# A reworked opening for a windowed-attention and feed-forward kernel: masks, row sums, key placement and loads of the first chunks

## The chip, the cores and the metric

The kernel runs on one NeuronCore of a Trainium2 chip. The core has engines that run side by side, each with its own queue of instructions taken in order: TensorE (PE, matrix products, with weight loads shown apart as PEld), VectorE (DVE), ScalarE (ACT), GpSimd (POOL) and SyncE (SP), which here only issues data transfers (DMA). SBUF is the working memory of 128 partitions; PSUM is the small memory into which TensorE writes.

The metric is device time in microseconds (us) of one execution. Times of instructions come from a profile of one execution; L275 is line 275 of the kernel's file.

## What is computed

```python
# attention: q, k, v are (8, 8, 576, 64) float32
scores = (1.0 / np.sqrt(64)) * np.matmul(q, k.transpose(0, 1, 3, 2))
mask = np.abs(pos[:, None] - pos[None, :]) <= 32
scores = np.where(mask, scores, -1000000000.0)
attn = np.exp(scores - np.max(scores, axis=-1, keepdims=True))
attn = attn / (np.sum(attn, axis=-1, keepdims=True) + 1e-09)
attn_out = np.matmul(attn, v)
# feed-forward on the 4608 tokens, heads side by side: x is (4608, 512)
h = x @ w_in            # (512, 2048)
g = np.maximum(0.01 * h, h)
out = g @ w_out         # (2048, 512)
```

Each token attends to the 65 tokens at most 32 positions away.

## The kernel before, in words

**Tiling.** Two heads form a pair (4 pairs per batch) and fill the 128 partitions together, 64 each. A batch of 576 tokens is cut into two halves of 288; a *chunk* i is one half of one pair, so there are 8 chunks per batch (0 to 3 the first half of pairs 0 to 3, 4 to 7 the second half) and 64 in all. Keys and values stand in block-diagonal buffers `kbd` and `vbd` (two of each, one per batch parity): per pair 9 blocks of 64 tokens, each 128 x 128 with one head in the upper left and the other in the lower right; the rest must be zero.

**One chunk.** `score(i)` multiplies key blocks with transposed queries into the PSUM tile `ps` (five matmuls, L275), ACT takes the exponential into `e` (L280), GpSimd multiplies with a mask of ones and zeros into `prob` (L282). `sums(i)` multiplies with a block-diagonal of ones, which gives the row sums already spread over the 64 partitions of a head (two matmuls, L304), and DVE takes the reciprocal of the 128 x 288 result (L309). `product(i)` multiplies with the value blocks into `x` (L320), and `scaled(i)` multiplies `x` with the reciprocals into `xT` (DVE, L334). `ps`, `s` and `x` have one PSUM buffer each, so the next chunk waits for the reader of the last.

**Feed-forward.** A *group* g is 288 tokens, 16 in all. `h_tile(g, f)` makes one 128-wide tile of h by four matmuls (L348), one for each pair's 128 columns of x, and ACT applies the leaky rectifier into `gT` (L355). `h_first` makes the first four tiles of a group with the pairs outermost, so that it can start before all pairs' `xT` are there. `o_tile(j)` makes 128 rows of the output by 16 matmuls (L390), evicted by ACT (L395) and stored through SP.

**Order of the work.** The order is written out by hand: every engine runs its instructions in the order of the program text, waiting on semaphores. For batches 0 and 1, q and k are cast to bf16 (`cast_qk`, L197), transposed on TensorE (`transposes`, L225) and evicted by ACT (L233 for q, L239 for k); `place_keys` then copies the keys into their blocks with DVE (L258). From batch 2 on, transposes are DMAs. Batch 0's q, k and v are all issued on SP (L79, L91), in the order q0 k0 q1 k1 v0 q2 k2 q3 k3 v1 v2 v3; after eight outstanding DMAs the next one waits for the first to land. The weights come in four chunks each through GpSimd's queue (L448, L452), cast to bf16 on the way. `keep_busy` (L402) issues matmuls whose result nobody reads.

The opening mixes casts, transposes, scores, sums and products of chunks 0 to 3 with the first feed-forward tiles. Batch 1's loads are released by a one-element memset on GpSimd (L75, `behind`), because SP would otherwise issue them early. `second_half` runs chunks 4 to 7 between the tiles of group 0. `second_pair(p)` transposes pair p of batch 1 between tiles of group 1 and, by `turn` (a counter of slots of four output matmuls), between the first output matmuls; from there a list of due times, `due`, decides in which slot the next chunk's `step` is placed.

Of the kernel before, what the change touches and what calls it, by code (L numbers as in the profile page):

```python
# [9 lines left out]
FP32 = mybir.dt.float32  # L10
# [6 lines left out]
def kernel(  # L17
# [50 lines left out]
    def load_qk(b, p, behind=None):  # L68
# [3 lines left out]
        for into, src, name in ((qf, q, "qf"), (kf, k, "kf")):  # L72
# [5 lines left out]
            if b < BY_DMA:  # L78
                nc.sync.dma_start(out=t, in_=heads.rearrange("a (p c) d -> p a (c d)", c=RUN))  # L79
            else:  # L80
                nc.sync.dma_start(
                    out=t.rearrange("p a (g e) -> p a g e", g=3),
                    in_=heads.rearrange("a (g p c) d -> p a g (c d)", g=3, c=2),
                )
            into[b, p] = t

    def load_v(b, p):

        t = fload.tile([128, NB, D], FP32, name=f"vf{p}")
        for a in range(2):  # L90
            nc.sync.dma_start(  # L91
                out=t[64 * a:64 * a + 64],
                in_=v[b, 2 * p + a].rearrange("(c p) d -> p c d", p=64),
            )
        vf[b, p] = t

    load_qk(0, 0)
    load_qk(0, 1)
    load_v(0, 0)
    load_qk(0, 2)  # L100
    load_qk(0, 3)
    for p in range(1, NPAIR):
        load_v(0, p)
# [33 lines left out]
    clear(vbd[0], 2)  # L137
# [20 lines left out]
    nc.gpsimd.memset(vbd[0][:, 3], 0.0)  # L158
    win_f = win.rearrange("p c m i -> p c (m i)")

    def make_mask(hf):
# [4 lines left out]

    NPROB = 6
# [5 lines left out]
    nc.scalar.activation(  # L173
        out=ps[:, 512:512 + HALF], in_=zero.to_broadcast([128, HALF]), func=AF.Copy,
    )
# [23 lines left out]
    def cast_v(b, p, on_act=False):  # L199
        for a in range(2):  # L200
            r = slice(64 * a, 64 * a + 64)
            if on_act:
                nc.scalar.activation(out=vbd[b % 2][r, p, :, r], in_=vf[b, p][r], func=AF.Copy)  # L203
            else:
                nc.gpsimd.tensor_copy(out=vbd[b % 2][r, p, :, r], in_=vf[b, p][r])  # L205
# [12 lines left out]
    def transposes(b):  # L218

        qT[b] = attn.tile([128, NPAIR, S], BF16, name="qT")  # L220
        for p in range(NPAIR):
            for which, src in (("q", qb), ("k", kb)):
# [14 lines left out]
                else:  # L237
                    kT = kt.tile([128, S], BF16, name="kT")
                    nc.scalar.activation(  # L239
                        out=kT.rearrange("p (i c) -> p i c", c=RUN),  # L240
                        in_=tp.rearrange("p c i -> p i c"), func=AF.Copy,
                    )
                    unplaced.append((b, p, kT))
                yield

    unplaced, landing = [], []

    def place_keys():

        while landing and landing[0][0] <= state["done"]:  # L250
            unplaced.append(landing.pop(0)[1:])
        while unplaced:
            b, p, kT = unplaced.pop(0)
            for a in range(2):
                r = slice(64 * a, 64 * a + 64)
                to = kbd[b % 2][r, p, :, r]
                if b < BY_DMA:
                    nc.vector.tensor_copy(out=to, in_=kT[r].rearrange("p (n j) -> p n j", j=64))  # L258
                else:
                    nc.vector.tensor_copy(  # L260
                        out=to.rearrange("p n (m c) -> p n c m", c=2),
                        in_=kT[r].rearrange("p (c n m) -> p n c m", c=2, n=NB),
                    )
# [6 lines left out]
    def score(i):  # L270
        b, hf, p = where(i)
        by_c = qT[b][:, p].rearrange("p (c i) -> p c i", c=2)
        for n_, blocks in enumerate(WIN[hf]):
            for blk, i0, n in blocks:
                nc.tensor.matmul(  # L275
                    ps_v[:, n_, :, i0:i0 + n], kbd[b % 2][:, p, blk],
                    by_c[:, :, hf * EVEN + i0:hf * EVEN + i0 + n], start=True, stop=True,
                )
        e = attn.tile([128, 2 * HALF], BF16, name="e")
# [15 lines left out]
    def sums(i):  # L295
# [14 lines left out]
        probs[i][2] = r  # L310

# [57 lines left out]
    def h_first(g):  # L369

        hs = [mmps.tile([128, 512], FP32, name="mm", tag="mm") for _ in range(4)]
        yield hs[0]
        for c in range(DMC):
            for f in range(4):
                h_mms(g, f, hs[f], (c,))
            if c == DMC - 1:
                for f in range(4):
# [19 lines left out]

    def keep_busy(t, lo, n):


        for _ in range(n):
            nc.tensor.matmul(  # L402
                t[:, lo:lo + 224], ones_bd, mask[0].rearrange("p n c i -> p (n c i)")[:, 0:224], start=False, stop=False,
                skip_group_check=True,
            )
# [14 lines left out]
    def step():  # L420
# [7 lines left out]
        weighted(i)  # L428
# [218 lines left out]
```

## Time and profile before

| | us |
|---|---|
| runs (three) | 318.51, 319.07, 320.56; median 319.07 |
| profiled execution, whole | 320.23 |
| its span, first to last instruction | 318.5 |
| PE busy | 303.2 (95%) |
| DVE busy | 218.2 (69%) |
| POOL busy | 191.6 (60%) |
| ACT busy | 182.6 (57%) |
| reciprocals L309 | 125.2, 64 of 1956 ns |
| mask multiplies L282 | 81.5, 64 of 1274 ns |
| SP and DMA: q or k load of 288 KB, issue to landing (median) | 4.5 and 5.0 |

The profile's page cuts the span into 40 slices and gives each engine's busy share in tenths, lists the chain of work that ended last, groups instructions by line with mean duration and the idle time ahead of them, and lists DMA issues. The timeline gives instructions in order of time: start, duration, engine, line, what is written from what. In the chain, "issue" is time in which an engine waited for nothing that the profile shows, SPq is SP's queue, and "DMA kf" is time until a transfer of keys landed.

### The profile page before, as it was taken

The page shows a single profiled execution, that of the slowest core. Times are in us where ns is not written, and L with a number is a line of the kernel's source. Part 1 is how long each engine was busy: PE and PEld are TensorE (multiplying, and loading weights), DVE is VectorE, ACT ScalarE, POOL GpSimd, SP SyncE. Part 2 cuts the span into 40 slices and gives each one's busy share as a digit, 9 for nine tenths or more (in the row PEclk, how much of TensorE's full clock was granted, in tenths as well). Part 3 has the DMA queues.
Part 4 walks back from the last instruction along what each step waited for, and adds up shares of the span by engine and source line. Part 5 has one row for each costly group of instructions (what it writes and reads, how often), then busy time and mean ns, then how long its engine had stood idle before and what let it go on. Part 6 is the DMA issues. An engine that isn't in the chain of part 4 may idle for free.

```text
span 318.5 us, 6474 instructions
## 1 busy us (share of the span) xinstructions
PE 303.2 (95%) x2449; PEld 204.3 (64%) x2449; DVE 218.2 (69%) x259; ACT 182.6 (57%) x393; POOL 191.6 (60%) x251
## 2 busy tenths in 40 slices
PE   2679998999999999999999999999999999999996
PEld 1467774585765858576765858576665858576653
DVE  5678955869655997688755997688745988565100
ACT  7577698474652828374652828375552837464531
POOL 7798963974546866686546866586637866330000
PEclk9999999999999999999999999999999999999999
DMA  8999999997999995399735995399733430000101
GB/s 179 211 186 218 267 250 203 250 206 181 216 242 196 231 206 150 82 251 203 155 76 127 238 227 136 75 223 232 162 76 104 109 70 33 35 35 2 66 31 71
DMA packets 108400, 49.46 MB, mean 155 GB/s; under 512 B 68816, under 2 KB 103888, under 8 KB 108368
## 3 DMA queue, kind: packets, MB, share of 16 engines
q1 hardware_dynamic: 104144, 44.84, 66.8%
q0 software_dynamic: 4224, 4.19, 8.0%
q8 instruction: 19, 0.31, 0.4%
q14 instruction: 13, 0.11, 0.1%
HBM read 36.70 MB, written 9.44 MB: 145 GB/s over the span
## 4 chain that ended last, share of the span: by engine, by line
PE 89%; DMA 3%; DVE 2%; SPq 1%; POOL 1%; ACT 1%; issue 1%; DVEq 0%; ACTq 0%
PE mm L348 39%; PE mm L390 38%; PE x L320 5%; PE ps L275 4%; DMA kf<-in_k_dram 3%; PE s L301 2%; DVE r L309 2%; SPq L79 1%; POOL w_in_bf L448 1%; DVE xT L334 1%; PE tp L225 1%; PE s L304 1%; ACT vbd L203 0%; SPq L91 0%; POOL prob L282 0%
## 5 line engine op out<-in xcount | busy, mean ns | idle before, releaser
L309 DVE RECIPROCAL r<-s 128x288 f32<-128x288 f32 x64 | 125.2, 1956 | 56.5 <-PE s L301 53.3
L282 POOL TENSOR_TENSOR prob<-e,mask 128x576 bf16<-128x576 bf16 x64 | 81.5, 1274 | 87.8 <-ACT e L280 41.1
L348 PE MATMUL mm<-xT,w_in_bf 128*128 128x288 bf16 x1024 | 134.0, 286 | 0.3
L390 PE MATMUL mm<-w_out_bf,gT 128*128 128x512 bf16 (+2 forms) x592 | 130.4, 373 | 0.2 <-DMA w_out_bf<-in_moe_w_out_dram 0.2
L355 ACT ACTIVATE gT<-mm 128x288 bf16<-128x288 f32 x256 | 101.4, 412 | 24.8 <-PE mm L348 8.5
L348 PEld LDWEIGHTS <-w_in_bf 128*128 128x128 bf16 x1024 | 98.4, 98 | 24.8 <-issue 0.6
L390 PEld LDWEIGHTS <-gT 128*128 128x128 bf16 x592 | 56.3, 98 | 59.6 <-issue 0.3
L395 ACT ACTIVATE o_sb<-mm 128x512 f32<-128x512 f32 (+2 forms) x37 | 21.7, 586 | 92.0 <-PE mm L390 92.0
L280 ACT ACTIVATE e<-ps 128x576 bf16<-128x576 f32 x64 | 41.4, 648 | 9.4 <-PE ps L275 9.2
L197 POOL CAST kb<-kf 96x384 bf16<-96x384 f32 (+1 forms) x56 | 35.5, 656 | 4.6 <-DMA kf<-in_k_dram 4.6
L205 POOL CAST vbd<-vf 64x576 bf16<-64x576 f32 x50 | 34.5, 689 | 1.8 <-DMA vf<-in_v_dram 0.4
L334 DVE TENSOR_TENSOR xT<-x,r 128x288 bf16<-128x288 f32 x64 | 29.3, 458 | 8.2 <-PE x L320 1.2
L260 DVE COPY kbd<-kT 64x576 bf16<-64x576 bf16 x48 | 32.3, 672 | 0.3
L275 PE MATMUL ps<-qT,kbd 128*128 128x128 bf16 (+2 forms) x320 | 26.5, 215 | 1.8 <-DVE kbd L258 1.2
L275 PEld LDWEIGHTS <-kbd 128*128 128x128 bf16 x320 | 21.0, 100 | 10.6 <-DVE kbd L258 1.5
L320 PE MATMUL x<-prob,vbd 128*128 128x128 bf16 (+2 forms) x320 | 26.0, 213 | 1.3 <-ACT vbd L203 0.7
L197 POOL CAST qb<-qf 96x384 bf16<-96x384 f32 x48 | 24.5, 538 | 0.0
L320 PEld LDWEIGHTS <-vbd 128*128 128x128 bf16 x320 | 20.6, 99 | 3.9 <-ACT vbd L203 1.8
L292 DVE TENSOR_TENSOR both<-prob 128x288 bf16<-128x288 bf16 x52 | 19.7, 380 | 0.9
L301 PE MATMUL s<-both,ones_bd 128*128 128x288 bf16 x52 | 14.9, 286 | 0.0
L258 DVE COPY kbd<-kT 64x576 bf16<-64x576 bf16 x16 | 7.1, 444 | 8.7 <-ACT kT L239 8.6
L225 PE MATMUL tp<-ident,qb 96*128 96x96 bf16 x48 | 4.4, 243 | 6.2 <-DVE qb L197 6.2
(43 smaller groups left out, 86.6 us busy)
## 6 DMA issues: line engine op xcount, KB each, us to landing
qf<-in_q_dram SPq DMA_DIRECT2D x32, 288.0 KB, 4.5
kf<-in_k_dram SPq DMA_DIRECT2D x32, 288.0 KB, 5.0
vf<-in_v_dram SPq DMA_DIRECT2D x64, 144.0 KB, 4.2
out_dram<-o_sb SPq DMA_DIRECT2D x35, 256.0 KB, 3.6
w_in_bf<-in_moe_w_in_dram POOLq DMA_DIRECT2D x4, 512.0 KB, 8.6
w_out_bf<-in_moe_w_out_dram POOLq DMA_DIRECT2D x4, 512.0 KB, 16.8
qT<-qb SPq DMA_TRANSPOSE x24, 4.1
kT<-kb SPq DMA_TRANSPOSE x24, 3.2
```

Source lines behind the costliest of these rows:

```text
L197: eng.tensor_copy(out=to, in_=tok)
L205: nc.gpsimd.tensor_copy(out=vbd[b % 2][r, p, :, r], in_=vf[b, p][r])
L260: nc.vector.tensor_copy(out=to.rearrange("p n (m c) -> p n c m", c=2), in_=kT[r].rearrange("p (c n m) -> p n c m", c=2, n=NB),)
L275: nc.tensor.matmul(ps_v[:, n_, :, i0:i0 + n], kbd[b % 2][:, p, blk], by_c[:, :, hf * EVEN + i0:hf * EVEN + i0 + n], start=True, stop=True,)
L280: nc.scalar.activation(out=e, in_=ps[:, P0:P0 + 2 * HALF], func=AF.Exp, scale=scale)
L282: nc.gpsimd.tensor_mul(pr.rearrange("p n c i -> p (n c i)"), e, mask[hf].rearrange("p n c i -> p (n c i)"),)
L309: nc.vector.reciprocal(r, s)
L320: nc.tensor.matmul(x_v[:, :, i0:i0 + n], vbd[b % 2][:, p, blk, :], pr[:, n_, :, i0:i0 + n], start=(blk == parts[0][1]), stop=(blk == parts ...
L334: nc.vector.tensor_mul(place(i), x, r)
L348: nc.tensor.matmul(h[:, 0:HALF], w_in_bf[:, c, ts(f, 128)], xT[:, c, ds(g * HALF % RING, HALF)], start=(c == 0), stop=(c == DMC - 1),)
L355: nc.scalar.activation(out=gT[:, f, ds(g * HALF % RING, HALF)].rearrange("p (i c) -> p i c", c=2), in_=h[:, 0:HALF].rearrange("p (c i) -> ...
L390: nc.tensor.matmul(o[:, lo:hi], gT[:, f, ds(128 * j % RING, 128)], w_out_bf[:, f, lo:hi], start=(f == 0), stop=(f == FFC - 1),)
```

## The change

All of it concerns the first two batches.

- **Loads.** Batch 0's queries go on SP, its keys on ACT's queue; its values follow, first blocks 0 to 4 of all pairs, then blocks 5 to 8. Batch 1's sixteen loads move in the text from the middle of the opening to after group 0.
- **Masks.** For chunks 0 to 3 TensorE first writes a tile `outside` (0 inside the window, -1e9 outside) into `ps` through an identity matrix, then adds the scores to it; the exponential goes straight into `prob`. From chunk 4 on GpSimd multiplies as before.
- **Row sums.** For chunks 0 to 3 `prob` is the stationary operand and two columns of ones move, so that sums come out by token row (96 rows, 6 columns); DVE takes the reciprocal of 96 x 6, copies it out 64-fold in fp32 (`wide`), and three fp32 matmuls with an identity turn it back into 128 x 288, which ACT copies to SBUF.
- **Keys.** For batches 0 and 1 the transposed keys are evicted from PSUM into their blocks directly, one head by ACT, the other by DVE.
- **Order.** The opening is rewritten, `keep_busy` is gone, the first `h_first` makes three tiles, value casts of batch 0 are all on GpSimd in two parts, two of the clears of `vbd` move to DVE. Batch 1's transposes and the first due times move to later slots, and chunks 9 to 11 have their sums made a step earlier.

```diff
-    load_qk(0, 0)
-    load_qk(0, 1)
-    load_v(0, 0)
-    load_qk(0, 2)
-    load_qk(0, 3)
-    for p in range(1, NPAIR):
-        load_v(0, p)
+    for p in range(NPAIR):
+        load_qk(0, p, k_eng=nc.scalar)
+    NB1 = NB // 2 + 1
+    for p in range(NPAIR):
+        load_v(0, p, 0, NB1)
+    for p in range(NPAIR):
+        load_v(0, p, NB1, NB)
...
+    make_mask(0)
+    outside = const.tile([128, 2, HALF], BF16)
+    nc.vector.tensor_scalar(
+        out=outside.rearrange("p n t -> p (n t)"),
+        in0=mask[0].rearrange("p n c i -> p (n c i)"),
+        scalar1=1e9, scalar2=-1e9, op0=ALU.mult, op1=ALU.add,
+    )
...
-                    kT = kt.tile([128, S], BF16, name="kT")
+                    nat = tp.rearrange("p c i -> p i c")
                     nc.scalar.activation(
-                        out=kT.rearrange("p (i c) -> p i c", c=RUN),
-                        in_=tp.rearrange("p c i -> p i c"), func=AF.Copy,
+                        out=kbd[b % 2][0:64, p, :, 0:64], in_=nat[0:64], func=AF.Copy,
                     )
-                    unplaced.append((b, p, kT))
+                    nc.vector.tensor_copy(out=kbd[b % 2][64:128, p, :, 64:128], in_=nat[64:128])
...
+        if i < NPAIR:
+            for n_ in range(2):
+                nc.tensor.matmul(
+                    ps[:, ds(P0 + n_ * HALF, HALF)], ident, outside[:, n_], start=True, stop=False,
+                    skip_group_check=True,
+                )
...
+        if i < NPAIR:
+            pr = prob[:, i % NPROB]
+            nc.scalar.activation(
+                out=pr.rearrange("p n c i -> p (n c i)"), in_=ps[:, P0:P0 + 2 * HALF],
+                func=AF.Exp, scale=scale,
+            )
+            probs[i] = [pr, None, None]
+            return
...
+    def sums_flat(i):
+        pr = probs[i][0].rearrange("p n c i -> p n (c i)")
+        sT = mmps.tile([128, 512], FP32, name="mm", tag="mm")
+        for c in range(3):
+            for n in range(2):
+                nc.tensor.matmul(
+                    sT[0:96, ds(2 * c, 2)], pr[:, n, ds(96 * c, 96)], ones_bd[:, 0:128:64],
+                    start=(c == 0 and n == 0), stop=True, skip_group_check=True,
+                )
+        rT = recip.tile([96, 3, 2], FP32, name="rT")
+        nc.vector.reciprocal(rT.rearrange("p c a -> p (c a)"), sT[0:96, 0:6])
+        wide = recip.tile([96, 3, 2, 64], FP32, name="wide")
+        nc.vector.tensor_copy(out=wide, in_=rT.unsqueeze(3).to_broadcast([96, 3, 2, 64]))
+        probs[i][1] = wide
+    def sums_spread(i):
+        wide = probs[i][1]
+        r = xps.tile([128, HALF], FP32, name="s")
+        for c in range(3):
+            nc.tensor.matmul(
+                r[:, ds(96 * c, 96)], wide[:, c].rearrange("p a d -> p (a d)"),
+                ident_f[0:96, 0:96], start=True, stop=True,
+            )
+        probs[i][2] = recip.tile([128, HALF], FP32, name="r")
+        nc.scalar.activation(out=probs[i][2], in_=r, func=AF.Copy)
...
     cast_qk(0, 0, nc.vector)
-    make_mask(0)
+    first_pair()
+    nc.vector.memset(vbd[0][:, 2], 0.0)
     cast_qk(0, 1, nc.vector)
     first_pair()
+    load_w_in(0, 512)
+    score(0)
+    nc.vector.memset(vbd[0][:, 3], 0.0)
+    cast_qk(0, 2, nc.vector)
     first_pair()
...
+    sums_flat(0)
+    cast_qk(0, 3, nc.vector)
+    load_w_in(512, 1024)
+    make_mask(1)
+    sums_spread(0)
+    sums_flat(1)
+    score(2)
+    first_pair()
+    sums_spread(1)
+    cast_v(0, 0, n1=NB1)
+    sums_flat(2)
+    product(0)
+    scaled(0)
     score(3)
+    sums_spread(2)
+    cast_v(0, 1, n1=NB1)
     product(1)
     scaled(1)
+    h0 = h_first(0, 3)
+    next(h0)
+    next(h0)
+    sums_flat(3)
+    load_w_in(1024, 1536)
+    cast_v(0, 2, n1=NB1)
     product(2)
     scaled(2)
+    next(h0)
+    sums_spread(3)
+    cast_v(0, 3, n1=NB1)
+    score(4)
+    product(3)
+    scaled(3)
+    load_w_in(1536, 2048)
+    next(h0)
+    load_w_out(0)
+    next(h0)
+    cast_v(0, 0, n0=NB1)
+    score(5)
     load_w_out(1)
     load_w_out(2)
+    cast_v(0, 1, n0=NB1)
+    load_w_out(3)
     score(6)
+    cast_v(0, 2, n0=NB1)
+    cast_v(0, 3, n0=NB1)
...
     second_half()
+    for p in range(NPAIR):
+        load_qk(1, p, nc.gpsimd if p == 0 else None)
+    for p in range(NPAIR):
+        load_v(1, p)
...
-        if f in (7, 11):
-            second_pair((f - 7) // 4)
+        if f == 14:
+            second_pair(0)
...
-    due = [O_US * n for n in (4, 7, 10, 12)]
+    due = [O_US * n for n in (10, 12, 14, 15)]
...
-        if turn == 1:
-            second_pair(2)
-        if turn == 2:
-            score(9)
-        if turn == 4:
-            second_pair(3)
+        if turn in (2, 6, 9):
+            second_pair({2: 1, 6: 2, 9: 3}[turn])
+        if turn in (3, 5):
+            score(8 + turn // 4)
+        if turn == 9:
+            sums(8)
+        if turn == 10:
             cast_v(1, 0, on_act=True)
```

## The prediction

> **What bounds the kernel now.** I read the page first, then the chain of waits in order of time, then the timeline of the first 65 us. From the page:
>
> ```profile
> PE   2679998999999999999999999999999999999996
> DMA  8999999997999995399735995399733430000101
> PE 89%; DMA 3%; DVE 2%; SPq 1%; POOL 1%; ACT 1%; issue 1%; DVEq 0%; ACTq 0%
> ```
>
> TensorE is full in every slice but the first four (8 us each) and the last. 89% of the chain is TensorE, so behind the opening a microsecond is worth one only where TensorE is made to wait. The chain through the opening:
>
> ```profile
> 5.83 9.66 DMA kf<-in_k_dram
> ...
> 15.54 0.82 POOL kb L197
> 16.36 2.35 POOL w_in_bf L448 x3
> ...
> 20.52 1.97 DVE r L309
> ...
> 23.91 1.88 DVE r L309
> ...
> 26.39 0.65 PE mm L348 x4
> ```
>
> The last keys land at 15.5; then GpSimd casts, issues three weight loads and masks; then VectorE's reciprocals follow each other until the fourth chunk of the first group can be multiplied at 26.39. These are what the change attacks. The timeline gives the durations I use (start, length, engine, line):
>
> ```profile
> 6.94 0.56 DVE L197 CAST qb<-qf 96x768 bf16<-96x768 f32 x1 [1.27 <-DMA qf<-in_q_dram]
> 7.78 0.91 DVE L258 COPY kbd<-kT 64x576 bf16<-64x576 bf16 x2 [0.28 <-ACT kT L239]
> 16.97 0.65 PE L275 MATMUL ps<-qT,kbd 128*128 128x96 bf16 x5
> 20.32 0.40 PE L275 MATMUL ps<-qT,kbd 128*128 128x96 bf16 x5
> 25.72 0.09 POOL L75 MEMSET qf<- 1x1 f32 x1
> 31.93 4.06 POOL L540 MEMSET kbd<- 128x1152 bf16 x4
> 64.16 1.63 PE L348 MATMUL mm<-xT,w_in_bf 128*128 128x288 bf16 x12
> ```
>
> To be seen: the second pair's query cast (6.94) runs before the first pair's keys are placed (7.78); the same five matmuls take 0.65 before about 19 us and 0.40 after; the memset that lets batch 1's loads go (25.72) stands six microseconds ahead of the long memsets of the other block buffers (31.93); from 64 us on (third group) the chain is TensorE without a gap.
>
> **What the Trainium skill says.** *TensorE: Matmul & The Clock Gate*, Part 1: the array runs at half clock until one window of about 3.4 us was busy. The trace agrees (0.65 against 0.40), though the clock row shows full speed. *DMA: Bandwidth & Descriptors*, Issuing engines are not separate DMA queues: a second issuing engine saves issue time only. The trace has 0.40 to 0.45 per q or k issue and shows no second ring. *FP8 and Floating Point Precision*, TensorE Precision Notes: true fp32 takes 4 passes; no fp32 matmul is in this trace. As prices: a VectorE read from PSUM is (120 + elements)/0.96 ns (*VectorE: DVE Perf Modes*, The TRN2 errata), 0.43 for the 288-element multiply that the trace shows at 0.46; a weight load is columns/1.2 ns (clock-gate page, LDWEIGHTS), 107 for 128 columns against 98 in the trace.
>
> **Method.** I walk the queues: each engine takes its instructions in program order, each starts 0.05 after the last thing it needs (cast ends 5.67, transposes start 5.72). Six transposes, or five score or value matmuls, take 0.48 of the array at half clock and 0.66 to their end (0.25 and 0.41 at full). Others, from the timeline: ACT eviction or exp 0.65, 0.43 for a gT; full reciprocal 1.96; multiply 0.46; mask multiply on GpSimd 1.27. Done for the kernel before with its own landing times, the walk puts the first group's fourth chunk at 26.5 (trace 26.39) and the third group at 64.7 (63.95).
>
> **The change part by part.**
>
> *Loads.* Keys go on ACT's queue, values after all of q and k. In the trace the first six microseconds of q and k move at 250 to 275 GB/s, later ones nearer 220: about 1.1 per 288 KB, plus some 1.7 to the signal. From 2.1, pair p is in at 2.1 + 2.2(p+1) + 1.7: 6.0, 8.2, 10.4, 12.6. Pair 0 comes later than before (queries 4.65), since two rings share the same engines; pair 3 three microseconds earlier. ACT's four issues push its table load and two clears to 6.1, which still precedes its first eviction.
>
> *Keys straight into blocks.* ACT's full eviction (0.65) plus two VectorE copies (0.91) become an ACT half (576 elements, 0.65) and a VectorE half from PSUM: (120 + 576)/0.96 = 0.72, an estimate from the page's price; 0.45 is its floor (one copy of today), 0.9 its top. But VectorE's half waits for ACT's half, and behind it in VectorE's queue stand a memset (0.5, a quarter of the 1.98 for 2304 elements) and the *next* pair's query cast, which before stood ahead. So each pair costs a whole round: cast 0.67, transposes 1.19 to their end, ACT 0.7, VectorE 0.77, memset 0.52, gaps 0.1: 3.95. Transposes start at 6.7, 10.6, 14.6 instead of 5.73, 7.55, 13.21. Landings no longer matter after pair 0.
>
> *Masks on TensorE.* Two 288-column matmuls per chunk (0.48 cold) ahead of the scores; GpSimd's 1.27 and its queueing go. Exp 0 ends at 13.4, against a masked result at 12.73 before.
>
> *Sums by token row.* Six small matmuls (weight load of 96 columns, 0.08 each: 0.5), reciprocal of 6 and broadcast copy of 384 (0.5 together, scaled from the 0.56 cast), three fp32 matmuls, ACT copy 0.4 replace two matmuls and the 1.96 reciprocal. The fp32 part: from below 0.3 (as bf16), from above 12 passes of 107 + 80 = 2.2; I take 1.1 (96 columns x 12 / 1.2 GHz, plus some loads). In sum a latency of 2.5 to 3, no shorter than 2.6 before; VectorE is freed of 1.5 each.
>
> *The fourth pair.* Its transposes stand on TensorE behind chunk 0's spread, which needs its broadcast (17.8), behind chunk 1's sums and chunk 2's scores: 20.4. Then ACT 22.4, VectorE 23.2, masks and scores 23.9, exp 24.6, sums 26.2, broadcast 26.8, spread 28.1, copy 28.6, multiply 29.1: fourth chunk at 29.2, 2.8 later than 26.39. The dummy matmuls are gone, but the array is dense from 18.7, so I take full clock from 22 (16 gives -0.5, 28 gives +1.6).
>
> *The order behind it.* Score 6 stands right behind score 5 and ahead of tile 3, and waits for an exp that ACT runs after three gT: tile 3 starts at 31.5. Before reached the same place at 27.17 with 0.73 more done (tile 3 and one sum): 5.1 behind. Then chunk 5's sums wait 1.0 for chunk 4's reciprocal, chunk 6's wait 1.5 for GpSimd, whose queue now has w_out issues (0.80 each) and second-half value casts between the masks: the second group starts at 42.8 instead of 35.2, 7.6 behind.
>
> *Batch 1's loads.* The memset that frees SP for them now comes after GpSimd's last mask (41.3) and six memsets (6.1): 47.5 instead of 25.8. All sixteen loads of q, k and v move past the weights on SP. First queries land 4.2 later; their cast ends at 52.4, and TensorE, ready at 50.5, waits 2; the keys cost 1.2 more, the next pair 0.6, and the four attention steps, squeezed between the last 24 output matmuls (24 x 0.216 = 5.2) though each needs 2.4 of VectorE, 2 to 3. Third group at 76.7 against 64.7 in the same walk: **12.0 later**. Nothing in the gap-free part after it gives this back, and it has the same work.
>
> The sum against the profiled execution: span 318.5 + 12.0, with 1.7 around it (320.23), is 332.2; that execution lies 1.2 above the median, so 319.07 + 12.0 = **331.1**.
>
> **Rivals.** Within 1% (3.2 us) cannot be told from no change.
>
> 1. *Same mechanism, cheap new operations*: fp32 at 0.3 per spread, VectorE half at 0.45, sums at 0.3, clock full from 16. Third group at 71.1, +6.4: 325.5. For it: no row excludes any of the five. Against: five favourable values at once.
> 2. *Dear new operations*: 2.2 per spread, 0.9 half, sums 0.8, cast 0.9, full clock only at 28: third group at 84.7, +20: 339. For it: weight loads of fp32 may not overlap, and the dummies were there to warm the array.
> 3. *Faster, through the loads*: today's chain has 9.66 on the last keys. Were the landings what holds the pairs, pair 3 at 12.6 instead of 15.5, less the reciprocals' 4 x 1.5 on VectorE and with no mask hop, would bring chunk four some 3.5 forward: 315.6. It decides if the round per pair falls below the 2.2 between landings; the queues give 3.95, so this needs VectorE's half not to wait for ACT and its cast to run ahead, which the program order excludes.
> 4. *No effect*: the opening loses what later slack returns. The trace has only about 1.5 of waiting between 27 and 64 us, so there is no such slack: 319.
>
> **Chances.** Forecast 0.62, cheap 0.17, dear 0.13, loads 0.05, no effect 0.03. Faster 0.05, within 1% 0.03, slower 0.92. The range runs from the cheap case's edge, 325, to 338, just short of the dear bound.
>
> **What would show it.** Transposes of pairs 1 and 2 near 10.6 and 14.6, led by VectorE; pair 3's after 19; fourth chunk of the first group at 27 to 31; a TensorE gap before score 6; batch 1's first q load issued after 45; third group at 71 to 82. I am wrong if VectorE's casts run ahead of ACT's evictions, if pairs follow the landings, or if batch 1's loads are out before 40.

## The result, and the profile after

Over four runs each the changed kernel takes 337.56 us (median) and the kernel before 319.35: 1.057 times as long, with a 95% interval of 1.050 to 1.064. The forecast was 331.1 with a range to 338.0, so the median lies 0.4 inside the range's end, and two of its four runs (338.47, 339.44) lie outside. The profiled execution of the changed kernel took 338.47 and has a span of 336.8.

The page of the changed kernel, TensorE's and the transfers' busy tenths and the share of the chain of waits by engine:

```profile
PE   1598797978999999899999999999999999999995
DMA  8990989999999999929993499559952521010101
PE 77%; POOL 6%; DVE 4%; DMA 4%; issue 4%; ACT 3%; SPq 0%; ACTq 0%; POOLq 0%; DVEq 0%
```

The slices are 8.4 us long. TensorE is now short of full in five slices past the third (to 84 us) and again in the seventeenth (from 135 us), and the fourth slice of the transfers is empty: from 25 to 34 us they moved 1 GB/s.

The chain of waits of the changed kernel (start, length, what) shows who sets the opening:

```profile
8.09 0.76 DVE kbd L250
8.85 0.17 issue
9.01 0.54 DVE vbd L499
9.55 0.42 DVE qb L203
9.97 0.05 issue
10.02 0.68 PE tp L232 x6
...
43.34 3.99 POOL kbd L573 x4
47.33 2.00 POOL vbd L573 x2
49.33 0.04 POOL qf L75
```

One round per pair is there: VectorE's half of the keys, a memset, the next query cast, then the transposes. Further down stand the six long memsets ahead of the one that releases batch 1's loads. TensorE's timeline (start, length, line, written from read, in brackets the wait ahead) gives the clock:

```profile
23.63 0.66 PE L282 MATMUL ps<-qT,kbd 128*128 128x96 bf16 x5
28.19 1.44 PE L349 MATMUL s<-ident_f,wide 96*128 96x96 f32 x6
29.41 0.66 PE L282 MATMUL ps<-qT,kbd 128*128 128x64 bf16 x5
31.15 0.53 PE L392 MATMUL mm<-xT,w_in_bf 128*128 128x288 bf16 x3 [0.24 <-DVE xT L378]
31.51 0.40 PE L282 MATMUL ps<-qT,kbd 128*128 128x64 bf16 x5
33.08 0.40 PE L282 MATMUL ps<-qT,kbd 128*128 128x64 bf16 x5 [1.16 <-ACT e L296]
33.31 0.65 PE L392 MATMUL mm<-xT,w_in_bf 128*128 128x288 bf16 x4
```

Five score matmuls take 0.66 until 29.4 and 0.40 from 31.5: the array (TensorE's grid of multipliers) was slow to about 30. The page's row of the granted clock reads full speed all the while, so a slow opening has to be read from the lengths of like matmuls; where the clock falls back later, the row does show it (experiments 2 and 5). The first group's fourth chunk is at 31.15 (26.39 before), and score 6 waits 1.16 ahead of tile 3. Last, VectorE late in the run:

```profile
128.83 0.46 DVE L378 TENSOR_TENSOR xT<-x,r 128x288 bf16<-128x288 f32 x1
131.57 1.05 DVE L261 COPY kbd<-kT 64x576 bf16<-64x576 bf16 x2 [2.28 <-DMA kT<-kb]
132.64 1.18 DVE L308 TENSOR_TENSOR both<-prob 128x288 bf16<-128x288 bf16 x1
```

VectorE waits 2.28 for a key transpose of batch 3, with the next chunk's sums queued behind it. In the profile of the kernel before, the same copy follows chunk 22's multiply without a wait:

```profile
113.09 0.46 DVE L334 TENSOR_TENSOR xT<-x,r 128x288 bf16<-128x288 f32 x1
113.47 1.33 DVE L260 COPY kbd<-kT 64x576 bf16<-64x576 bf16 x2
```

**A common ruler.** Below, *lag at chunk i* is the start of chunk i's multiply into `xT` in one profiled execution, less its start in the profile of the kernel before. Times are medians; the ratio to the kernel before, measured beside each, has its 95% interval.

| kernel | lag at chunk 0 | 3 | 4 | 7 | 8 | 16 | 28 | time, ratio |
|---|---|---|---|---|---|---|---|---|
| changed kernel | 7.2 | 4.8 | 7.7 | 9.7 | 16.8 | 15.7 | 17.7 | 337.56, 1.050 to 1.064 |
| 1 casts earlier | 5.3 | 2.3 | 5.3 | 7.6 | 14.8 | 13.7 | 13.7 | 334.32, 1.044 to 1.055 |
| 2 dummies | 6.6 | 3.0 | 6.0 | 8.3 | 15.7 | 14.6 | 14.6 | 336.64, 1.050 to 1.056 |
| 3 full reciprocals | 8.6 | 3.9 | 7.8 | 8.3 | 15.6 | 14.5 | 16.4 | 335.06, 1.047 to 1.053 |
| 4 early loads | 7.0 | 3.6 | 6.5 | 8.9 | 13.2 | 12.1 | 12.1 | 332.83, 1.040 to 1.044 |
| 5 = 1 + 3 + 4 | 6.3 | 1.1 | 5.5 | 5.7 | 10.0 | 9.0 | 11.6 | 330.80, 1.029 to 1.039 |
| 6 = 5 + order | 6.2 | 1.8 | 4.6 | 8.1 | 8.7 | 8.6 | 8.6 | 329.16, 1.027 to 1.034 |
| 7 = 5 + dummies | 5.9 | 1.0 | 4.5 | 4.7 | 9.0 | 7.9 | 7.9 | 328.47, 1.026 to 1.031 |
| 8 = 7 + order as before | 5.6 | 1.3 | 1.6 | 2.7 | 3.1 | 3.0 | 3.0 | 324.02, 1.010 to 1.022 |

The changed kernel's loss comes in four stretches: 4.8 up to chunk 3 (the first group can be finished), 4.9 from there to chunk 7 (the second group), 6.0 to chunk 16, and 2.0 at about 130 us.

### The profile page after: what moved, and what is told of

The parts are those of the page before. It is cut to its first block, busy times and chain, and to the rows that moved or that the text cites. A ratio compares the mean times of both kernels' runs of the same rounds, so it can differ in the third digit from the quotient of the medians.

```text
span 336.8 us, 6518 instructions
## 1 busy us (share of the span) xinstructions
PE 309.2 (92%) x2455; PEld 211.3 (63%) x2476; DVE 213.6 (63%) x259; ACT 179.2 (53%) x388; POOL 191.1 (57%) x260
## 4 chain that ended last, share of the span: by engine, by line
PE 77%; POOL 6%; DVE 4%; DMA 4%; issue 4%; ACT 3%; SPq 0%; ACTq 0%; POOLq 0%; DVEq 0%
PE mm L434 32%; PE mm L392 32%; PE x L364 4%; PE ps L282 4%; POOL prob L298 2%; PE s L317 2%; DMA kf<-in_k_dram 2%; PE s L349 2%; PE tp L232 1%; DMA qf<-in_q_dram 1%; POOL kbd L573 1%; DVE r L325 1%; DMA kT<-kb 1%; POOL vbd L212 1%; DVE kbd L261 1%
## 5 line engine op out<-in xcount | busy, mean ns | idle before, releaser
L325 DVE RECIPROCAL r<-s 128x288 f32<-128x288 f32 x60 | 117.4, 1956 | 55.3 <-PE s L317 49.8
L298 POOL TENSOR_TENSOR prob<-e,mask 128x576 bf16<-128x576 bf16 x60 | 76.6, 1277 | 98.3 <-ACT e L296 50.0
L434 PE MATMUL mm<-w_out_bf,gT 128*128 128x512 bf16 (+2 forms) x571 | 129.0, 373 | 1.1
L296 ACT ACTIVATE e<-ps 128x576 bf16<-128x576 f32 x60 | 38.8, 647 | 10.8 <-PE ps L282 10.8
L212 POOL CAST vbd<-vf 64x576 bf16<-64x576 f32 (+2 forms) x64 | 40.3, 630 | 2.1
L203 POOL CAST kb<-kf 96x384 bf16<-96x384 f32 (+1 forms) x56 | 34.6, 639 | 12.1 <-DMA kf<-in_k_dram 12.1
L261 DVE COPY kbd<-kT 64x576 bf16<-64x576 bf16 x48 | 31.7, 661 | 2.8 <-DMA kT<-kb 2.5
L308 DVE TENSOR_TENSOR both<-prob 128x288 bf16<-128x288 bf16 x52 | 22.1, 426 | 2.6 <-POOL prob L298 1.9
L250 DVE COPY kbd<-tp 64x576 bf16<-64x576 bf16 x8 | 6.1, 761 | 13.1 <-ACT kbd L247 13.0
```

The costliest lines, as they stand in the source:

```text
L203: eng.tensor_copy(out=to, in_=tok)
L212: nc.gpsimd.tensor_copy(out=to, in_=src)
L261: nc.vector.tensor_copy(out=kbd[b % 2][r, p, :, r].rearrange("p n (m c) -> p n c m", c=2), in_=kT[r].rearrange("p (c n m) -> p n c m", c=2 ...
L296: nc.scalar.activation(out=e, in_=ps[:, P0:P0 + 2 * HALF], func=AF.Exp, scale=scale)
L298: nc.gpsimd.tensor_mul(pr.rearrange("p n c i -> p (n c i)"), e, mask[hf].rearrange("p n c i -> p (n c i)"),)
L325: nc.vector.reciprocal(r, s)
```

## The experiments

### Four parts of the change undone or covered, one at a time

**1. Query casts one pair earlier.**

```diff
     cast_qk(0, 0, nc.vector)
-    first_pair()
-    nc.vector.memset(vbd[0][:, 2], 0.0)
     cast_qk(0, 1, nc.vector)
     first_pair()
+    cast_qk(0, 2, nc.vector)
+    nc.vector.memset(vbd[0][:, 2], 0.0)
+    first_pair()
...
-    nc.vector.memset(vbd[0][:, 3], 0.0)
-    cast_qk(0, 2, nc.vector)
+    cast_qk(0, 3, nc.vector)
+    nc.vector.memset(vbd[0][:, 3], 0.0)
     first_pair()
...
     sums_flat(0)
-    cast_qk(0, 3, nc.vector)
```

> The changed kernel with every query cast of batch 0 put one pair earlier (and the memsets of vbd behind it), so that no cast is queued behind VectorE's half of an eviction; nothing else. Theory (the round per pair, led by VectorE's queue): the second and third pairs' transposes start at about 8.2 and 10.8 instead of 10.02 and 13.86, the first group's fourth chunk at 28.8 instead of 31.15, the second group near 42.2, and the end comes 2.5 earlier: 335.1 against 337.6. Rival (the half-clock array is what holds everything from 15 us on, so earlier transposes only move waiting): transposes earlier, fourth chunk within 0.7 of 31.15, end within 0.8. Rival (landings set the pairs): transposes not before 9.5 and 13.

Measured: transposes of the second and third pair at 7.90 and 10.58, fourth chunk at 28.70, 334.32, so 3.2 less than the changed kernel. Two lines of TensorE's timeline of this kernel:

```profile
7.90 0.66 PE L232 MATMUL tp<-ident,qb 96*128 96x96 bf16 x6 [0.72 <-DVE qb L203]
10.58 0.66 PE L232 MATMUL tp<-ident,qb 96*128 96x96 bf16 x6 [0.28 <-DVE qb L203]
```

In VectorE's timeline of this kernel the casts ahead of them (7.28 and 9.97) wait 1.51 and 1.32 for their queries to land, so the pairs now follow the landings. The lag is smaller by 2.5 at chunk 3 and by 2.0 at chunk 16. The round per pair is shown as a cause; the slow array did not absorb the gain. The late wait for keys is missing from this profile too, although no load of batch 1 was moved.

**2. Dummies in TensorE's waits.** Each is a matmul of 224 columns into `ps`.

```diff
     first_pair()
+    keep_busy(ps, 0, 13)
...
+    keep_busy(ps, 0, 9)
     nc.vector.memset(vbd[0][:, 3], 0.0)
...
     sums_flat(0)
+    keep_busy(ps, 0, 4)
```

> The changed kernel with 26 matmuls whose result nobody reads put into the waits of TensorE before the second and third pair's transposes (13 and 9) and before the first spread (4); nothing else. Theory (cold array to 30 us because no window was full): five score matmuls take 0.40 instead of 0.66 from 19 us or earlier, three h matmuls 0.5 instead of 0.93, the first group's fourth chunk at 28.6 instead of 31.15, end 2.3 to 2.6 earlier: 335.1. Rival (TensorE's speed is not what ends the waits there, VectorE's rounds are): durations fall but the fourth chunk stays within 0.7 of 31.15 and the end within 0.8 of 337.6. Rival (the dummies delay the transposes): slower than 337.6.

Measured: 336.64; the fourth chunk came 1.7 earlier (29.43), and the lag at chunk 16 is smaller by 1.1, less than half of what I expected at the end. TensorE's timeline of this kernel says why in part:

```profile
6.97 2.63 PE L447 MATMUL ps<-mask,ones_bd 128*128 128x224 bf16 x13
10.86 0.40 PE L282 MATMUL ps<-qT,kbd 128*128 128x96 bf16 x5
15.90 0.54 PE L447 MATMUL ps<-mask,ones_bd 128*128 128x224 bf16 x4 [0.83 <-ACT prob L289]
18.85 0.66 PE L282 MATMUL ps<-qT,kbd 128*128 128x96 bf16 x5
25.23 0.93 PE L392 MATMUL mm<-xT,w_in_bf 128*128 128x288 bf16 x3
```

The array was fast at 10.9, and slow again at 18.9, after waits of 1.03, 0.36, 0.83 and 0.43; it stayed slow to 27 without a wait. The granted clock of the trace agrees: 0.52 on average from 17.7 to 28.0. The second and third lot of dummies could not fill the waits they were meant for, because they write `ps` and so had to wait (1.03 and 0.83) until ACT had read the scores there. This run is thus no test of an array that stays fast; 7 is.

**3. Full reciprocals instead of sums by token row.** Each `sums_flat(i)` becomes `sums(i)`, and the four `sums_spread(i)` go.

> The changed kernel with chunks 0 to 3 summed as before: two matmuls with the block of ones and the 128 x 288 reciprocal on VectorE, no sums by token row, no fp32 matmuls, no copy by ACT. Theory: the latency of the two ways is about equal (1.96 + 0.48 against 0.46 + 0.6 + 1.35 + 0.41), so the first group's fourth chunk stays near 31.2, the array has 1.1 to 1.3 less work per chunk, the second group comes about 1.2 earlier (43.5) and the end 1.2: 336.4. Rival (the fp32 matmuls at half clock are a main cost of the change): 3 or more earlier. Rival (the reciprocals' 4 x 1.5 on VectorE are a true saving): 1.5 or more later, 339.

Measured: 335.06, lag at chunk 16 smaller by 1.2. The size of the effect on the lag is the expected one; the median gained more, 2.5, but the profiled execution, 336.91, was the longest of its four runs and has the late wait for keys. Sums by token row cost rather than save. The reason I read from the timelines is that the two ways take about as long, but TensorE, which from 19 to 30 us has no time to spare, gets one of these more for each chunk. TensorE's timeline of the changed kernel:

```profile
17.20 1.59 PE L349 MATMUL s<-ident_f,wide 96*128 96x96 f32 x6 [0.86 <-DVE wide L341]
20.91 1.56 PE L349 MATMUL s<-ident_f,wide 96*128 96x96 f32 x6
```

In the chain the second of them takes 1.36. The six small matmuls of the row sums and the two of the full sums are about equal (0.61 and 0.69 by the two timelines), so this comes on top.

**4. Batch 1's loads early.**

```diff
     load_w_out(0)
+    for p in range(NPAIR):
+        load_qk(1, p, nc.gpsimd if p == 0 else None)
     next(h0)
...
     cast_v(0, 3, n0=NB1)
+    for p in range(NPAIR):
+        load_v(1, p)
...
     second_half()
-
-    for p in range(NPAIR):
-        load_qk(1, p, nc.gpsimd if p == 0 else None)
-    for p in range(NPAIR):
-        load_v(1, p)
```

> The changed kernel with batch 1's q and k loads (and the memset that releases them) directly behind the first w_out issue on GpSimd instead of behind its six long memsets, and v's loads behind the last value cast of batch 0. Theory (loads released late cost TensorE's waits at 53 to 57 and again the late key transposes at 126 to 141, because transfers stood idle from 25 to 34 and the backlog is worked off only later): first q issue of batch 1 near 34 instead of 49.4, third group 3.5 earlier (score of chunk 14 near 78), the late wait of 2.0 gone, end 5 to 6 earlier: 332. Rival (only the first of these, the late stall has a cause of its own): 3.5 earlier, 334. Rival (the casts of keys behind the long memsets and the late slots hold the batch anyway): within 1 of 337.6.

Measured: first q issue of batch 1 at 32.91, 332.83, so 4.7 less, and no late wait. (The late wait is missing from 1 and 2 as well, where these loads stayed late, so this run doesn't show that early loads remove it.) TensorE's first transposes of batch 1 no longer wait. Its timeline, first of this kernel, then of the changed one:

```profile
51.73 0.42 PE L232 MATMUL tp<-ident,qb 96*128 96x96 bf16 x6
51.99 0.42 PE L232 MATMUL tp<-ident,kb 96*128 96x96 bf16 x6
```

```profile
53.36 0.43 PE L232 MATMUL tp<-ident,qb 96*128 96x96 bf16 x6 [0.62 <-DVE qb L203]
54.84 0.43 PE L232 MATMUL tp<-ident,kb 96*128 96x96 bf16 x6 [1.05 <-POOL kb L203]
```

Of the 3.6 at chunk 16 only 2.8 came after chunk 7. Chunk 3 was 1.2 earlier already, although nothing ahead of it was edited: here the array was fast at 28.0 (the spread that starts there takes 0.85), in the changed kernel still slow at 28.2 (1.44). A single profile can thus be off by about 1 through the moment at which the array speeds up.

### The parts together

**5. Three undone at once**: the edits of 1, 3 and 4.

> The changed kernel with three undone at once: casts of batch 0 one pair earlier, full reciprocals for chunks 0 to 3, batch 1's q and k loads behind the first w_out issue. By the multiplies into xT, chunk 16 of the changed kernel is 15.7 behind the kernel before, and each alone took 2.0, 1.2 and 3.6 of it. Theory (they stand one behind the other on the path): sums add, chunk 16 is 8.9 behind, no late wait, 328.5. Rival (they cover each other, since keys of batch 1 wait for GpSimd's long memsets however early the rest is): chunk 16 at 11 or more behind, 331 or more. What is left in either case is in the order of the work from score 4 on and in batch 1's late slots.

Measured: lag at chunk 16 is 9.0, so 6.7 less than in the changed kernel; the three alone add up to 6.8. The time, 330.80, missed my 328.5. The profiled execution, 331.84, has the late wait for keys again: the lag goes from 9.0 to 11.6 behind chunk 22. The two quickest of its four runs took 329.51 and 329.77; whether they have the wait isn't known. TensorE's timeline of this kernel has the array fast and then slow again:

```profile
22.98 0.40 PE L364 MATMUL x<-prob,vbd 128*128 128x96 bf16 x5 [1.85 <-DVE xT L378]
24.84 0.66 PE L282 MATMUL ps<-qT,kbd 128*128 128x64 bf16 x5
```

The granted clock was 1.00 from 20.8 to 24.2, a stretch in which TensorE was busy for 1.55 of 3.40, and 0.50 from there to 34.4.

**6. The order behind the opening.** On top of 5, among others:

```diff
-    score(6)
     cast_v(0, 2, n0=NB1)
...
         if f == 3:
             sums(4)
+            score(6)
...
-    due = [O_US * n for n in (10, 12, 14, 15)]
+    due = [O_US * n for n in (5, 8, 11, 13)]
```

> The last kernel, and three more of its order changed: score 6 behind the tile of h that it held up, the last w_in and the first w_out issue ahead of GpSimd's first mask (GpSimd stands idle there for 10), and batch 1's transposes and first due times moved forward to tiles 9 and 13 of group 1 and to slots 5, 8, 11 and 13. Theory (the order behind the opening costs about 1 for score 6, 1 to 2 for the masks and 2 for the squeezed slots): 4 to 5 earlier than the last kernel, 324. Rival (what is left was lost in the opening itself): within 1 of the last kernel.

Measured: 329.16, only 1.6 less than 5; my theory as put fell. The lags tell it in two halves: from chunk 7 to chunk 8, over the first steps of batch 1, this kernel loses 0.6 where 5 lost 4.3, but up to chunk 7 it lost 2.4 more. The slots gave up to 3.7, where I expected 2; moving score 6 back was harmful, because chunk 6's mask came to stand behind four value casts on GpSimd, and TensorE waited 2.0. GpSimd's, then TensorE's timeline of this kernel:

```profile
34.75 1.76 POOL L212 CAST vbd<-vf 64x256 bf16<-64x256 f32 x4
36.60 2.50 POOL L298 TENSOR_TENSOR prob<-e,mask 128x576 bf16<-128x576 bf16 x2
```

```profile
37.91 0.41 PE L320 MATMUL s<-prob,ones_bd 128*128 128x288 bf16 x2 [2.00 <-POOL prob L298]
38.16 3.12 PE L392 MATMUL mm<-xT,w_in_bf 128*128 128x288 bf16 x16
41.07 0.66 PE L364 MATMUL x<-prob,vbd 128*128 128x64 bf16 x5
```

The sixteen h matmuls behind that wait took 3.12 instead of 2.12: the array had become slow again. What the earlier w_in and w_out issues did was not told apart from this.

**7. Three undone, with dummies** (48 in all: `keep_busy(ps, 0, 16)` behind `sums(0)` and behind `score(3)`, and smaller ones).

> The changed kernel with the three undone as before (casts earlier, full reciprocals, early loads of batch 1), and 48 matmuls whose result nobody reads in TensorE's waits: 2 before the second pair's transposes, 16 before chunk 1's sums, 16 before product 1, 8 before product 3, 6 before score 6. Without them the array was at half clock (five matmuls in 0.61 to 0.66) to 20.6 and again from 24.4 to 34.3, with some 8 us of work in it. Theory (each wait of 2 or more lets the array fall back, and the work after it is long again): five matmuls at 0.40 from 20 on without a return, eight h matmuls at 1.14 instead of 2.12, chunk 16 at 5 behind the kernel before instead of 9.0, end 4 earlier than the three undone, 326.8. Rival (in the waits something else, mostly VectorE's reciprocals, sets the pace, and a fast array only waits longer): chunk 16 at 8 or more, within 1.5 of 330.8.

Measured: the array was fast from 16.8 on without a return, and yet the lag at chunk 16 is 7.9, 1.1 less than in 5: by the lag the rival was right (8 or more), to 0.1. The time fell by 2.3, more than the rival's 1.5, but the profile of 5 has the late wait and this one hasn't. TensorE's timeline of this kernel:

```profile
13.99 2.94 PE L447 MATMUL ps<-mask,ones_bd 128*128 128x224 bf16 x16 [0.26 <-ACT prob L289]
17.26 0.40 PE L282 MATMUL ps<-qT,kbd 128*128 128x96 bf16 x5
```

VectorE's, the multiply of chunk 3 and the reciprocal of chunk 4, names what sets the pace:

```profile
26.84 0.46 DVE L378 TENSOR_TENSOR xT<-x,r 128x288 bf16<-128x288 f32 x1 [0.58 <-PE x L364]
31.03 1.96 DVE L325 RECIPROCAL r<-s 128x288 f32<-128x288 f32 x1 [3.73 <-PE s L320]
```

VectorE stands idle for 3.73, since chunk 4's sums are written behind score 6 and a tile. From there on one reciprocal follows the other, 2.5 to 2.8 per chunk, and most of what TensorE saves is waited for.

**8. The order from score 4 on as before**, on top of 7:

```diff
     cast_v(0, 3, n1=NB1)
-    score(4)
-    keep_busy(ps, 0, 8)
-    product(3)
-    scaled(3)
     load_w_in(1536, 2048)
-    next(h0)
     load_w_out(0)
+    score(4)
     for p in range(NPAIR):
         load_qk(1, p, nc.gpsimd if p == 0 else None)
+    score(5)
+    keep_busy(ps, 0, 3)
+    product(3)
+    scaled(3)
+    next(h0)
+    sums(4)
     next(h0)
     cast_v(0, 0, n0=NB1)
-    score(5)
...
-        if f == 3:
-            sums(4)
...
-        if f == 14:
-            second_pair(0)
+        if f in (9, 13):
+            second_pair((f - 9) // 4)
```

Further down the slots of batch 1's first steps go back as well, as in 6.

> The kernel of three undone with dummies, and now the order from score 4 on as in the kernel before: scores 4 and 5 ahead of product 3, chunk 4's sums ahead of the fourth chunk of the first group, score 6 behind it, the last w_in and first w_out issue ahead of GpSimd's first mask, batch 1's pairs at tiles 9 and 13 of group 1, score 8 behind the last tile, first due slots 5, 8, 11, 13, no sums a step early. What stays of the change: loads, keys straight into blocks, masks on TensorE, values cast on GpSimd in two parts. In the kernel without it the multiplies into xT were 1.0 behind the kernel before at chunk 3, 4.5 at chunk 4, 4.7 at chunk 7 and 9.0 at chunk 8. Theory (3.5 lost to chunk 4's sums behind score 6 and a tile, 3 to 4 to the late slots): chunk 4 at 1.5, chunk 7 at 1.7, chunk 16 at 2 behind, end 322. Rival (GpSimd's and the transfers' state of the changed opening holds chunks 4 to 12, whatever the order): chunk 16 at 6 or more, 326 or more.

Measured: lag 1.6 at chunk 4, 2.7 at chunk 7, 3.0 at chunk 16, 324.02, two more than expected. The theory holds, for chunk 4 to 0.1, for the lags behind it to 1. In VectorE's timeline of this kernel, the two lines that answer those of 7:

```profile
27.22 0.46 DVE L378 TENSOR_TENSOR xT<-x,r 128x288 bf16<-128x288 f32 x1 [1.23 <-PE x L364]
27.83 1.96 DVE L325 RECIPROCAL r<-s 128x288 f32<-128x288 f32 x1 [0.15 <-PE s L320]
```

So 4.9 of the 15.7 were the order of the work from chunk 4 on; how it divides between chunk 4's sums, the scores, the issues of weights and loads and the slots was not taken apart. Nor were the 3.0 that remain (loads, keys straight into blocks, masks, value casts on GpSimd).

### Two parts alone, in the kernel before

**9. Masks on TensorE for chunks 0 to 3.** `score` gets the branch of the change for these chunks; all else is the kernel before.

> The kernel before with one part of the change alone: chunks 0 to 3 masked by adding a tile of 0 and -1e9 to the scores on TensorE, the exponential straight to prob, no GpSimd multiply for them. Theory (the part is not what costs: a hop of 1.27 goes, 0.48 or 0.25 of matmuls comes, and VectorE's reciprocals set the pace): the third chunk's reciprocal 0.4 earlier, end 0 to 0.5 earlier, 319.2 against 319.5. Rival (eight matmuls of 288 columns on a cold array are part of the loss): 1.5 to 2 later. Rival (the mask hop was on the path four times): 2 or more earlier.

Measured: 323.12 (ratio 1.006 to 1.015), so 3.4 longer than the kernel before beside it, more than any of the three theories had, and not for the rival's reason. The multiplies are 0.7 *ahead* at chunks 1 to 7 and still at 22; then VectorE waits for keys of batch 3, as in the changed kernel, and the lag is +1.1. VectorE's timeline of this kernel:

```profile
112.39 0.46 DVE L352 TENSOR_TENSOR xT<-x,r 128x288 bf16<-128x288 f32 x1
114.75 1.04 DVE L262 COPY kbd<-kT 64x576 bf16<-64x576 bf16 x2 [1.91 <-DMA kT<-kb]
```

The profiled execution took 321.37 and is the shortest of the four; the others took 322.86 to 324.50, which its trace doesn't explain. So masks on TensorE cost nothing in the opening by this profile, and yet the kernel is longer by more than the profile has; what of this they cost in the changed kernel is open.

**10. The loads alone**: q on SP's queue, k on ACT's, values behind them, pair 0's value cast behind score 1.

> The kernel before with the loads of the change alone: queries on SP's queue, keys on ACT's, all values behind them (whole, not in two parts), and the value cast of pair 0 on GpSimd moved behind score 1, since its data come later. Theory (the landings of the last pair are not what binds once GpSimd's and VectorE's queues are counted): the last keys land near 13 instead of 15.5, but GpSimd has the first values to cast before them, the first multiply comes 0.8 later, end 0.5 to 1 later: 320.3. Rival (the last landing is what the opening waits for, as the chain of waits has it with 9.66): the first group's fourth chunk 1 to 2.5 earlier, 317.5.

Measured: 321.61 (1.004 to 1.009), lag 1.4 from chunk 1 to the end. GpSimd's timeline of this kernel: the last key cast starts at 16.16, later than before (15.54), straight behind the value casts and without a wait for its keys:

```profile
14.72 1.38 POOL L202 CAST vbd<-vf 64x576 bf16<-64x576 f32 x2
16.16 0.82 POOL L194 CAST kb<-kf 96x768 bf16<-96x768 f32 x1
```

The 9.66 on the last keys in the chain of the kernel before were therefore not 9.66 to be won. The value cast stands there because I had moved it with the loads, so the run shows the loads and this move together.

### The late wait for keys

It is in the profiles of the changed kernel, 3, 5 and 9, and not in 1, 2, 4, 6, 7, 8 and 10. I tried to take it away by placing keys that come by DMA one step later, once on 9, once on the changed kernel:

```diff
-        landing.append((8 * (b - 1) + 4 + p, b, p, kT))
+        landing.append((8 * (b - 1) + 5 + p, b, p, kT))
```

> The kernel before with the masks of chunks 0 to 3 on TensorE, as in the run of that part alone, and the keys that come by DMA (batch 2 on) put into their blocks one step later. In that run the multiplies into xT were 0.7 ahead up to chunk 22, and then VectorE waited 1.9 for batch 3's keys and chunk 24 was 2.2 behind. Theory (the part is worth 0.7, and it was a key transpose landing late behind SP's full queue that took it back and more): no wait of VectorE for a key transpose above 0.5, chunks 16 to 60 all 0.5 to 0.8 ahead, end 0.7 earlier than the kernel before: 318.9 against 319.6. Rival (the late keys hold up the score itself, so a later copy only moves the wait to TensorE): 321 or more. Rival (the part costs time of its own): chunk 16 not ahead.

> The changed kernel with nothing but the keys that come by DMA put into their blocks one step later. Theory (the wait of 2.3 of VectorE for batch 3's keys at about 130 us, with the sums queued behind it, is what adds 2.0 between chunks 22 and 26): chunk 16 still 15.7 behind the kernel before, chunks 24 to 60 the same 15.7, end 2 earlier than the changed kernel, 335.4. Rival (TensorE waits for those keys in any case): chunks 26 to 60 at 17 or more, 337.5.

Measured: 323.09 (1.009 to 1.013) and 339.14 (1.059 to 1.063), no gain in either, so the rivals were right that a later copy only moves the wait. VectorE's wait for the transposes is gone in both, but now TensorE's scores wait for the copies (from 60 us on 13 times in each, 5.9 in all). From the waits of the second of these kernels between 95 and 145 us:

```profile
PEld L282 <- DVE kbd L261: 1.6, 3, 0.9
PE ps L282 <- DVE kbd L261: 0.4, 1, 0.4
```

The line gives the wait in total, how often, and the longest. In the kernel of 9 with later copies chunk 16 is 0.1 behind the kernel before, not 0.7 ahead. In the other the lag grows from 15.9 at chunk 16 to 18.4 at chunk 60. So the copies cannot be later by a whole step: the keys would have to come earlier. What makes them late in some executions and not in others stays open. In the profile of 9, SP issued the first query transpose of batch 3 in 2.66 instead of 1.63, and its queue then ran 1.5 behind that of the kernel before, although the casts ahead of it were 0.7 earlier; that SP's full queue is the cause is argued from this, not shown.

## Why the prediction was right in sign and short in size

The mechanism of the prediction held: order, rounds and late loads put the third group back, and nothing after it gave time back. The size was short: 12.0 forecast, 18.2 measured. That the median still fell inside the range, by 0.4, is luck as much as foresight. Of the signs that I named, the rounds led by VectorE, pair 3's transposes after 19 (19.95), the gap ahead of score 6, the first load of batch 1 after 45 (49.39) and the start of the third group (78.18, named as 71 to 82) came; the fourth chunk, 31.15, came just behind its 27 to 31.

The sum ran 2.8 at the fourth chunk, 7.6 at the second group, 12.0 at the third. The lags at chunks 3, 7 and 16 are 4.8, 9.7 and 15.7, and 17.7 at chunk 28. (The third group itself starts 14.0 later, at 78.18 against 64.16 in TensorE's timelines, and then waits 1.56 more for chunk 11.)

- **Pair round, 3.95.** Right: 4.01 and 3.84 between the transposes (6.01, 10.02, 13.86), VectorE's half 0.76 against 0.77. The page *VectorE: DVE Perf Modes* (The TRN2 errata) gives (120 + 576)/0.96 = 725 ns as an estimate, and the trace agrees to 5%. Experiment 1 shows the cause; it was worth 2.0. All three starts were some 0.7 earlier than forecast (13.86, not 14.6, for the third), since pair 0's queries were there at 5.4 instead of 6.0. So 2.7 went missing between the third pair and the fourth chunk, of which the lag shows only 2.0.
- **Clock full from 22.** Wrong: about 30 (28 in experiment 4, with the same instructions ahead). I had reasoned that the array is dense from 18.7. It was, and stayed slow. *TensorE: Matmul & The Clock Gate* (Part 1) has full clock after one busy window of about 3.4 us. Thirteen dummies of 224 columns did it within 4 us (experiment 2); a denser eleven microseconds of transposes, two-column sums, fp32 spreads and scores did not, so here the measurement decides against the page as I read it. The prediction priced a clock at 28 with 1.6, which with the spreads' 1.1 below would make up the 2.7, though the two overlap, since a spread is itself shorter with a fast array. A clean number for the clock is missing: in experiment 2 the array fell back and the fourth chunk gained 1.7; in 7 it stayed fast, and the lag at chunk 16 gained 1.1 over 5.
- **fp32 spread, 1.1.** Short: 1.59, 1.36, 1.33 and 1.24 of the chain for the four, 1.1 more in sum. The page *FP8 and Floating Point Precision* (TensorE Precision Notes) has 4 passes; three matmuls of 96 columns in 4 passes are 0.96 at the 1.2 GHz that the clock page's Part 1 has for the half clock, an estimate. The trace has weight loads of 333 ns each there, which I had thought mostly hidden; that they are the rest is argued. The same three take 0.81 with a fast array (experiment 2, at 27.5).
- **Order behind it, 4.8 between fourth chunk and second group.** Right: 4.9. I named score 6, GpSimd's masks and reciprocals in a row. From experiment 7 to 8 the lag at chunk 4 falls by 2.9 and VectorE's wait there from 3.73 to 0.15; I put this down to one line of text, chunk 4's sums behind score 6 and a tile, but 8 moved scores and issues with it.
- **Batch 1's loads and slots, 4.4.** Short: 6.0. The loads came as described (first issue 49.39, memset 49.33 against 47.5), and their waits were smaller than I had them (2.1 instead of 3.8). The slots were dearer: 1.10, 0.30, 0.72 and 1.56 of waiting in the four attention steps, 3.7 instead of 2 to 3. My own terms didn't make 4.4: 3.8 and 2 to 3, less the 1.2 for which TensorE idles in this stretch of the kernel before, are 4.6 to 5.6. The measured ones, with 0.3 for an eviction of values and less the same 1.2, are 4.9; the other 1.1 is in no wait that the trace marks.
- **"Nothing in the gap-free part after it gives this back, and it has the same work."** It gave nothing back, but took 2.0 more: the part is free of gaps for TensorE, not of near misses. A transposed key that had landed just in time landed late.
- **Rivals.** The dear case at 339 came close by its time, with another mechanism: of its five dear values only the clock and, in part, the spread were so. Loads as a gain (315.6) fell by the result, and experiment 10, which has them with one cast moved, lost 1.4.

## What to carry to other kernels

Before a part of a change is judged, look at where its instructions stand in the queue of the engine that is in arrears: the order in which casts, sums, masks and releases of loads stand behind each other cost 10.5 of 15.7 by the lag at chunk 16 (2.0, 3.6 and 4.9 in experiments 1, 4 and 8). Of the new operations the sums by token row cost 1.2 (experiment 3); the others are in the 3.0 that were not taken apart. A gap-free stretch of the bounding engine doesn't mean slack in the queues that feed it: ask of each of them how late it may be. And a dense array is not yet a fast one: read the speed from the lengths of like matmuls, over the whole opening.

## What was not expected of the hardware

- The array stayed at half speed through eleven microseconds with almost no wait (18.8 to 29.9 in the changed kernel), but sped up within 3 us under 16 matmuls of 224 columns (experiment 7: 13.99 to 16.8). What it counts as busy was not tested.
- It falls back after short waits: in experiment 5, five score or value matmuls take 0.40 at 22.98 and 0.66 at 24.84; the longest wait of the 3.4 us at full clock was 1.85.
- Where VectorE's reciprocals follow each other, a fast array in place of a slow one (0.50 of the clock for 10.2 us in experiment 5) was worth 1.1 at chunk 16 (experiment 7).
